# Row-tiled transposes of k and r, late logits with the gate weights stationary, and re-searched due dates in a one-core kernel

## The chip, the core and the metric

The kernel runs on one core of a Trainium2 chip. The core has five engines that work side by side, each through its own list of instructions in order: TensorE (PE in the profile; its weight loads are PEld), VectorE (DVE), ScalarE (ACT), GpSimd (POOL) and SyncE (SP, which issues transfers). PE writes its results to eight PSUM banks, and DVE and ACT copy them from there. The metric is the device time of one execution in microseconds (us); lower is better.

## The reference

Three parts follow one another: a linear attention with decay, a dense feed-forward layer with softplus, and a mixture of eight experts in which every expert takes exactly 384 tokens.

```python
batch, n_heads, seq, head_dim = (4, 8, 768, 48)
for t in range(S):
    cur = np.einsum('bhd,bhe->bhde', u[None] * kt, vt)
    y[:, :, t] = np.einsum('bhd,bhde->bhe', rt, state + cur)
    state = w[None, :, :, None] * state + np.einsum('bhd,bhe->bhde', kt, vt)

h = x @ w_in                                             # 3072 x 384 by 384 x 2048
g = np.maximum(h, 0.0) + np.log1p(np.exp(-np.abs(h)))
x = g @ w_out

logits = x @ w_gate                                      # 3072 x 8
for idx in np.argsort(-logits.flatten()):                # best pair of token and expert first
    tok, e = (int(idx) // E, int(idx) % E)
    if assigned[tok] >= 0 or counts[e] >= cap: continue
    assigned[tok] = e
    counts[e] += 1
for e in range(E):
    out[assigned == e] = np.maximum(x[assigned == e] @ w1[e], 0.0) @ w2[e]
```

`w_in` and `w_out` come as float64 and are converted on the core.

## The kernel before

The 3072 tokens are cut into 24 steps of 128 (two batches of 64 positions each) and into 8 blocks of three steps (384 tokens).

**Attention, one step** (`attention(n)`). k and r, scaled by powers of the decay, lie in `ks` and `rs` with 128 tokens on the partitions; each head has 48 values in a slot of 64, so two heads make 128 columns. PE transposes them head pair by head pair: `tk` (L591) and `tq` (L595) are four transposes of 128x128 each, into one bank each. A transpose is a matmul in which the data are the stationary operand, loaded by a weight load, and the identity is streamed. Copies take the banks to SBUF: `kT` in one copy, and `ar` in two of 64 partitions (for the first three steps, called direct, `rT` in one). Then `prods` (L618) multiplies k by r inside the step in 64x64 tiles of the array, `masked` (L628, DVE) writes the masked products into the free half of `ar`, `fresh` (L649) makes the step's own state in 64x64 tiles, and `outs` (L710, 128x64 tiles) gives the output. f32 matmuls appear as two records each in the trace, transposes as one.

**Feed-forward.** `ffn1` (L862 for block 0 in f32; L869 in f16 with three products of high and low halves) and the softplus on ACT and DVE fill `G`, high half `gh` and low half `gl`. `ffn2` (L980 for block 0; L983 to L985 later) multiplies by `w_out`. Behind its 384 columns `w_out` carries eight columns of the product w_out times w_gate (made through L813, L825 and L830), so that logits come out with the layer's output. For the last twelve token tiles (`LATE`, blocks 4 to 7) the output is computed late, beside the selection of experts, and their logits are computed ahead of it by `late_logits`: per token tile 32 matmuls with 128x128 of G stationary and 16 (L910) or 8 (L911) gate columns streamed, and two small DVE instructions that add the parts into `LG`.

**Experts.** `select` finds the tokens of one expert after another (L1235, L1252 and many DVE instructions), `gather` fetches them, `experts` runs L1476 (up) and L1494 to L1496 (down), and the results are scattered to the output.

**What sets the order.** Every piece of work is an `op` with an engine (or a choice of engines), an expected duration, what it reads and writes, a due date and, on PE, the banks that it takes. `lay_out` plays these through in the planner's own time: of the items that could start within `SLACK` of the earliest it takes the one with the smallest due date plus `NUDGE`; an item marked `small` is kept with others of that mark, and entering them costs `SWITCH`. `BIAS` and `YIELD` weigh one engine against another where there is a choice. `keep_warm` puts filler matmuls (L187) where the planner's PE is idle. What results is a fixed list for each engine; on the chip the engines wait for one another by semaphores alone.

Of the kernel before, what the change touches and what calls it, by code (L numbers as in the profile page):

```python
# [21 lines left out]
def tile_kernel(ctx, tc, r, k, v, w, u, w_in, w_out, w_gate, w1, w2, out):  # L22
# [33 lines left out]
    SLACK = 65.403  # L56
    SAME = {"dve": 130.0, "act": 150.0}
    NBANK = 7
    BIAS = 1.611999999999999
    YIELD0 = 221.503  # L60
# [498 lines left out]
    def attention(n):  # L559
# [27 lines left out]
        b1, b2 = Bank("att"), Bank("att")  # L587

        def tk():
            for pr in range(HP):  # L590
                PE.transpose(b1.view(HP, 128)[:, pr, :], ks[:, 2 * pr:2 * pr + 2, :].rearrange("p a d -> p (a d)"), identf)  # L591

        def tq():
            for pr in range(HP):
                PE.transpose(b2.view(HP, 128)[:, pr, :], rs[:, 2 * pr:2 * pr + 2, :].rearrange("p a d -> p (a d)"), identf)  # L595

        def qcopy(eng, q):
            copied(eng, ar[q * 64:(q + 1) * 64, :, :, q, :], b2.view(HP, 2, 64)[q * 64:(q + 1) * 64])

        op("pe", 437.0, tk, r=[("ks", i), "ident"], w=[("kT", i)], due=due + 2, bank=b1)  # L600
        op(FROM_BANK, 0.0, lambda eng: copied(eng, kT, b1.view(HP, 128)), w=[("kT", i)], due=due + 2, bank=b1)
        op("pe", 437.0, tq, r=[("rs", i), "ident"], w=[("ar", i, 0), ("ar", i, 1)], due=due + 2, bank=b2)
        if direct:
            op(FROM_BANK, 0.0, lambda eng: copied(eng, rT, b2.view(HP, 128)), w=[("ar", i, 0), ("ar", i, 1)], due=due + 2, bank=b2)
        for q in range(0 if direct else 2):
            op(FROM_BANK, 0.0, lambda eng, q=q: qcopy(eng, q), w=[("ar", i, q)], due=due + 2, bank=b2)

        b3 = [Bank("att"), Bank("att")]

        def prods():
            for pr in range(HP):
                for b in range(2):
                    for q in range(2):
                        rows, cols = slice(q * 64, (q + 1) * 64), slice(b * 64, (b + 1) * 64)
                        PE.matmul(b3[q].view(HP, 64)[cols, pr], kT[rows, pr, cols], rT[rows, pr, cols] if direct else ar[rows, pr, b, q, :],  # L618
                                  start=True, stop=True)
# [983 lines left out]
```

## Time and profile before

| | us |
|---|---|
| median of 3 runs | 736.38 |
| lowest and highest of them | 735.86 and 738.37 |
| the profiled execution | 735.12 |
| its span, first to last instruction | 733.4 |
| PE busy | 720.7 |
| DVE busy | 602.8 |
| ACT busy | 401.9 |

The mean granted TensorE clock is 0.993 of full. Matmuls are pipelined, so their busy time counts overlaps: what one costs the engine's list is read as the distance from its start to the start of the next. A timeline row merges neighbouring instructions of one kind: xcount says how many, the first number when the first of them began.

### The profile page before, as it was taken

The page shows a single profiled execution, that of the slowest core. Times are in us where ns is not written, and L with a number is a line of the kernel's source. Part 1 is how long each engine was busy: PE and PEld are TensorE (multiplying, and loading weights), DVE is VectorE, ACT ScalarE, POOL GpSimd, SP SyncE. Part 2 cuts the span into 40 slices and gives each one's busy share as a digit, 9 for nine tenths or more (in the row PEclk, how much of TensorE's full clock was granted, in tenths as well). Part 3 has the DMA queues.
Part 4 walks back from the last instruction along what each step waited for, and adds up shares of the span by engine and source line. Part 5 has one row for each costly group of instructions (what it writes and reads, how often), then busy time and mean ns, then how long its engine had stood idle before and what let it go on. Part 6 is the DMA issues. An engine that isn't in the chain of part 4 may idle for free.

```text
span 733.4 us, 18232 instructions
## 1 busy us (share of the span) xinstructions
PE 720.7 (98%) x7175; PEld 472.5 (64%) x7175; DVE 602.8 (82%) x1634; ACT 401.9 (55%) x826; POOL 65.1 (9%) x107
## 2 busy tenths in 40 slices
PE   9999999999999999999999999999998999999996
PEld 8986666666666666766666666666664665666663
DVE  6999999997999878698789858887797799978630
ACT  3697597752885399566899702220344433534531
POOL 3000000000000000000010000001212322312211
PEclk9999999999999999999999999999999999999998
DMA  7997833356635510060410003343247467647900
GB/s 149 230 197 190 229 102 56 67 108 123 112 61 99 97 31 15 15 107 1 67 23 2 2 12 109 108 141 93 76 124 227 132 173 199 203 122 210 269 33 32
DMA packets 165013, 79.65 MB, mean 109 GB/s; under 512 B 132800, under 2 KB 158272, under 8 KB 164928
## 3 DMA queue, kind: packets, MB, share of 16 engines
q1 hardware_dynamic: 159216, 68.56, 40.5%
q0 software_dynamic: 3072, 9.44, 3.8%
q8 instruction: 56, 0.92, 0.5%
q10 hardware_dynamic: 2640, 0.49, 0.4%
q14 instruction: 29, 0.24, 0.1%
HBM read 60.37 MB, written 9.83 MB: 96 GB/s over the span
## 4 chain that ended last, share of the span: by engine, by line
PE 73%; DVE 11%; issue 7%; ACT 4%; DMA 2%; POOL 1%; SPq 1%; another core or an unknown queue 0%; POOLq 0%; DVEq 0%
PE bank L869 19%; PE bank L1476 8%; PE bank L983 7%; PE bank L984 7%; PE bank L985 7%; PE bank L980 4%; PE bank L1494 2%; PE bank L1496 2%; PE bank L1495 2%; PE bank L710 2%; DVE ar L628 2%; DMA vn<-v 1%; PE bank L862 1%; PE bank L1235 1%; PE bank L618 1%
## 5 line engine op out<-in xcount | busy, mean ns | idle before, releaser
L869 PEld LDWEIGHTS <-wi 128*128 128x128 f16 x1008 | 98.2, 98 | 65.3 <-issue 1.5
L869 PE MATMUL bank<-xt,wi 128*128 128x384 f16 x672 | 127.6, 326 | 0.0
L983 PE MATMUL bank<-wo,g 128*128 128x384 f16 (+1 forms) x240 | 79.3, 331 | 0.0
L984 PE MATMUL bank<-wo,g 128*128 128x384 f16 (+1 forms) x240 | 79.1, 330 | 0.0
L985 PE MATMUL bank<-wo,g 128*128 128x384 f16 (+1 forms) x240 | 79.1, 330 | 0.0
L886 DVE SCALAR_TENSOR_TENSOR gf<-bank,ta 128x384 f32<-128x384 f32 x112 | 61.6, 554 | 15.7 <-ACT ta L881 15.1
L1476 PE MATMUL bank<-g,w1h 128*128 128x384 f16 x384 | 74.0, 329 | 0.0
L869 PE MATMUL bank<-xs,wi 128*128 128x384 f16 x336 | 72.9, 326 | 0.0
L880 ACT ACTIVATE ta<-ta 128x384 f32<-128x384 f32 x128 | 66.2, 519 | 1.8
L879 ACT ACTIVATE ta<-bank 128x384 f32<-128x384 f32 x128 | 61.3, 479 | 10.6 <-PE bank L869 6.3
L881 ACT ACTIVATE ta<-ta 128x384 f32<-128x384 f32 x128 | 65.9, 519 | 2.0
L1494 PE MATMUL bank<-w2h,g 128*128 128x384 f16 x192 | 62.6, 326 | 0.0
L1496 PE MATMUL bank<-w2h,g 128*128 128x384 f16 x192 | 62.6, 326 | 0.0
L1495 PE MATMUL bank<-w2l,g 128*128 128x384 f16 x192 | 62.5, 326 | 0.0
L424 ACT ACTIVATE x2o<-bank 128x384 f16<-128x384 f32 x24 | 11.6, 489 | 88.7 <-PE bank L985 54.0
L1480 ACT ACTIVATE g<-bank 128x384 f16<-128x384 f32 x64 | 31.2, 489 | 46.9 <-PE bank L1476 27.8
L1476 PEld LDWEIGHTS <-w1h 128*128 128x128 f16 x384 | 35.7, 98 | 23.0 <-issue 1.3
L893 DVE SCALAR_TENSOR_TENSOR g<-gf,g 128x384 f16<-128x384 f32 x80 | 43.5, 553 | 3.0 <-ACT g L424 2.0
L1483 DVE SCALAR_TENSOR_TENSOR g<-bank,g 128x384 f16<-128x384 f32 x64 | 34.6, 549 | 11.0 <-ACT g L1480 10.9
L1476 PE MATMUL bank<-g,w1l 128*128 128x384 f16 x192 | 42.2, 329 | 0.0
L1399 POOL DMA_INDIRECT third<-x2d,idx x24 | 26.7, 1111 | 154.0 <-DVE si L1314 128.4
L1429 ACT ACTIVATE w2h<-mraw 128x768 f16<-128x768 f32 x32 | 26.9, 841 | 22.6 <-DMA mraw<-moe_w 18.8
(251 smaller groups left out, 1442.8 us busy)
## 6 DMA issues: line engine op xcount, KB each, us to landing
mraw<-moe_w SPq DMA_DIRECT2D x64, 384.0 KB
third<-moe_w_out SPq DMA_DIRECT2D x8, 768.0 KB
third<-moe_w_in SPq DMA_DIRECT2D x6, 768.0 KB
x2d<-x2o SPq DMA_DIRECT2D x48, 96.0 KB
vn<-v SPq DMA_DIRECT2D x47, 96.0 KB
rn<-r SPq DMA_DIRECT2D x46, 96.0 KB
kn<-k SPq DMA_DIRECT2D x46, 96.0 KB
X<-v SPq DMA_DIRECT2D x36, 96.0 KB
```

What stands on the lines that cost most here:

```text
L869: PE.matmul(ph, WF[:, f, a, kk, :], x[:, kk, :], start=(i == 0), stop=(i == 3 * KC - 1))
L879: op("act", 371.0, lambda: ACT.activation(ta, bank.view(BT), AF.Abs), w=[("ta", c)], due=due, bank=bank)
L880: op("act", 413.0, lambda: ACT.activation(ta, ta, AF.Exp, scale=-1.0), w=[("ta", c)], due=due)
L881: op("act", 413.0, lambda: ACT.activation(ta, ta, AF.Ln, bias=1.0), w=[("ta", c)], due=due)
L886: op("dve", 470.0, lambda: DVE.scalar_tensor_tensor(gf, bank.view(BT), 0.0, ta, op0=OP.max, op1=OP.add), r=[("ta", c)], w=[("gf", c)], due ...
L983: PE.matmul(p, gh[:, f, ts], WU[:, f, 0, :no], start=(f == 0), stop=False)
L984: PE.matmul(p, gh[:, f, ts], WU[:, f, 1, :no], start=False, stop=False)
L985: PE.matmul(p, gl[:, f, ts], WU[:, f, 0, :no], start=False, stop=(f == FC - 1))
L1476: PE.matmul(ph, a[:, kk, fs], XH[p][:, x0 + kk, :], start=(i == 0), stop=(i == 3 * KC - 1))
L1494: PE.matmul(po, h1h[:, f, js], w2h[:, fz, :], start=(f == 0), stop=False)
L1495: PE.matmul(po, h1h[:, f, js], w2l[:, fz, :], start=False, stop=False)
L1496: PE.matmul(po, h1l[:, f, js], w2h[:, fz, :], start=False, stop=(f == FB - 1))
```

## The change

**Transposes.** Instead of four transposes of k and four of r, each 128x128, there are sixteen (`turned`, L597): for k and r, each head pair and each half of the rows (64 tokens of one batch). The two halves lie in different row tiles of the array and write different banks, and each bank holds both k and r. The four or three copies after them change with it: `kT` in two copies of 128x4x64, `ar` in two copies of 128x4x128, in which each r column is written twice (for the direct steps `rT` in two of 128x4x64). All sixteen are one item, marked `small`, which waits for `ks` and `rs`; `prods` waits for all four copies.

**Late logits.** Per block (three token tiles at once) the gate columns are stationary: `gates` puts them into `WGC`, 32 columns for each of the 16 pieces of w_out (eight high, eight low, the rest zero). 32 matmuls (L927) stream 384 columns of `gh` or `gl` each, in four column tiles of 32; ACT or DVE copies the 128x384 result to `LT`, three transposes (L932) turn it, and one DVE sum over the eight parts writes `LG`. `more_room` waits for this group too.

**Due dates.** `SLACK`, `BIAS`, `YIELD0` and all of `NUDGE` have new values (the table is cut here).

```diff
-    SLACK = 65.403
+    SLACK = 116.403
-    BIAS = 1.611999999999999
-    YIELD0 = 221.503
+    BIAS = 1.4120000000000001
+    YIELD0 = 267.503
-        1: -143624, 2: 51762, 4: 34057, 14: -25973, 15: 68285, 16: 100082, 17: 135695, 18: -1000120765, 19: -234504, 20: -202425, 21:
+        1: -91444, 3: 999869890, 4: -146263, 6: 999897800, 17: 150794, 42: -181722, 53: -229368, 54: -84025, 55: -53118, 56: -96415, 57:
...
-        b1, b2 = Bank("att"), Bank("att")
-
-        def tk():
-            for pr in range(HP):
-                PE.transpose(b1.view(HP, 128)[:, pr, :], ks[:, 2 * pr:2 * pr + 2, :].rearrange("p a d -> p (a d)"), identf)
...
-        def qcopy(eng, q):
-            copied(eng, ar[q * 64:(q + 1) * 64, :, :, q, :], b2.view(HP, 2, 64)[q * 64:(q + 1) * 64])
-
-        op("pe", 437.0, tk, r=[("ks", i), "ident"], w=[("kT", i)], due=due + 2, bank=b1)
-        op(FROM_BANK, 0.0, lambda eng: copied(eng, kT, b1.view(HP, 128)), w=[("kT", i)], due=due + 2, bank=b1)
-        op("pe", 437.0, tq, r=[("rs", i), "ident"], w=[("ar", i, 0), ("ar", i, 1)], due=due + 2, bank=b2)
...
+        kr = [Bank("att"), Bank("att")]
+
+        def turned():
+            for a, src in enumerate((ks, rs)):
+                for pr in range(HP):
+                    for b in range(2):
+                        rows = slice(b * 64, (b + 1) * 64)
+                        PE.transpose(kr[b].view(2, HP, 64)[:, a, pr, :], src[rows, 2 * pr:2 * pr + 2, :].rearrange("p a d -> p (a d)"),
+                                     identf[rows, rows])
+
+        def rcopy(eng, b):
+            r = kr[b].view(2, HP, 64)[:, 1]
+            if direct:
+                copied(eng, rT[:, :, b * 64:(b + 1) * 64], r)
+            else:
+                copied(eng, ar[:, :, b], r[:, :, None, :].to_broadcast([128, HP, 2, 64]))
+
+        op("pe", 500.0, turned, r=[("ks", i), ("rs", i), "ident"], w=[("kT", i), ("ar", i, 0), ("ar", i, 1)], due=due + 2, bank=kr, small=True)
+        for b in range(2):
+            op({"act": 375.0, "dve": 340.0}, 0.0, lambda eng, b=b: copied(eng, kT[:, :, b * 64:(b + 1) * 64], kr[b].view(2, HP, 64)[:, 0]),
+               w=[("kT", i, b)], r=[("kT", i)], due=due + 2, bank=kr[b])
...
-                PE.matmul(p, gh[:, f, ts], WU[:, f, :, DM:], start=(f == 0), stop=False)
-                PE.matmul(p[:, :E], gl[:, f, ts], WU[:, f, 0, DM:], start=False, stop=(f == FC - 1))
+        def mm(qs):
+            for q in qs:
+                for a in range(2):
+                    for j in range(4):
+                        PE.matmul(b1.view(m * 128)[32 * j:32 * j + 32], WGC[:, 4 * q + j].rearrange("p a e -> p (a e)"), G[g][a][:, 4 * q + j, ts],
+                                  start=(q == 0 and a == 0), stop=(q == FC // 4 - 1 and a == 1), tile_position=(0, 32 * j))
+
+        def tr():
+            for i in range(m):
+                PE.transpose(b2.view(m, 128)[:, i], LT[:, i * 128:(i + 1) * 128], identf)
...
+            op("pe", 330.0 * len(qs), lambda qs=qs: mm(qs), r=[(a, g, f) for a in ("gh", "gl") for y in qs for f in range(4 * y, 4 * y + 4)] + keys,
+               due=due_ffn1(blk, 4 * q + 4) + 500.0 if last else due, bank=b1, small=True)
+        op({"act": 413.0, "dve": 470.0}, 0.0, lambda eng: copied(eng, LT[:, :m * 128], b1.view(m * 128)), w=["lt", ("wi", FC)], due=due, bank=b1)
+        op("pe", 115.0 * m, tr, r=["lt", "ident"], due=due, bank=b2)
```

Three places in the lists. First PE, where a step's transposes stand behind the late part of `ffn2` (names: `third` and `g` are G, `identf` the identity, the number behind a bank's name its place). Before:

```order
L984 MATMUL bank_85<-wo,third 128x392
L985 LDWEIGHTS third
L985 MATMUL bank_85<-wo,third 128x392
L591 MATMUL bank_82<-identf,ks_102 128x128 x4
L595 MATMUL bank_86<-identf,rs_100 128x128 x4
L649 MATMUL bank_81<-vn_96,ks_103 64x48
```

After, behind another step's `outs`; of the sixteen the first two of k and the last two of r are shown:

```order
L716 MATMUL bank_85<-X_97,ar_112 64x48 x16
L597 MATMUL bank_82<-identf,ks_103 128x64
L597 MATMUL bank_83<-identf,ks_103 128x64
...
L597 MATMUL bank_82<-identf,rs_101 128x64
L597 MATMUL bank_83<-identf,rs_101 128x64
L1005 LDWEIGHTS g_128
L1005 MATMUL bank_80<-wo,g_128 128x392
```

Eight full transposes became eight pairs that alternate between two banks, and a third tile shape (64x128) stands between the shapes around it.

Then PE at the end of the last block's late logits, ahead of the late `ffn2`. Before:

```order
L910 LDWEIGHTS g_4951
L910 MATMUL bank_85<-wo,g_4951 128x16
L911 LDWEIGHTS g_4952
L911 MATMUL bank_85<-wo,g_4952 128x8
L983 LDWEIGHTS g_128
L983 MATMUL bank_84<-wo,g_128 128x384
```

After:

```order
L927 LDWEIGHTS wo
L927 MATMUL bank_85<-g_5019,wo 32x384
L932 MATMUL bank_81<-identf,wi 128x128 x3
L1005 LDWEIGHTS g_128
L1005 MATMUL bank_86<-wo,g_128 128x384
```

G was loaded and the gate columns streamed; now the gate columns are loaded and G is streamed, and the transposes of the result stand between the first matmuls of the late `ffn2`, six of them ahead of each of the last two blocks' three.

Last ACT, which makes most copies of the steps. Before (one step's three copies, other work between them):

```order
L430 COPY ar_111<-bank_81 64x8x64
L430 COPY kT_110<-bank_82 128x512
L430 COPY ar_111<-bank_81 64x8x64
L424 ACTIVATE x2o_132<-bank_85 128x384
L430 COPY ar_112<-bank_86 64x8x64
```

After:

```order
L433 COPY kT_110<-bank_83 128x4x64
L433 COPY ar_112<-bank_83 128x4x128
L433 COPY ar_112<-bank_82 128x4x128
L433 COPY kT_110<-bank_82 128x4x64
L427 ACTIVATE xhl<-xf_115 128x384
```

Three copies a step became four; the elements per partition are 1536 in both.

Counted over the whole lists: PE changes between tile shapes 102 times before and 136 times after; behind the first matmul of `ffn2` of block 0 (L980 before, L1002 after) 63 and 88 times. Of the 24 steps' transposes, 132 of 192 stand behind that matmul before, and 17 of 24 steps' after. Fillers: 154 before, 143 of them ahead of that matmul; 213 after, 203 ahead of it.

## Rows read from the trace of the kernel before

**Rows 1.** the page: busy time of each engine, its share and its instructions
```profile
PE 720.7 (98%) x7175; PEld 472.5 (64%) x7175; DVE 602.8 (82%) x1634; ACT 401.9 (55%) x826; POOL 65.1 (9%) x107
```

**Rows 2.** busy time in stretches (from:to, length, engines, clock, DMA share, GB/s)
```profile
60.00:80.00 20.00, 19.61 (x265) 13.81 (x265) 19.19 (x38) 15.25 (x33) 0.00 (x0) 1.00 0.79 205
80.00:100.00 20.00, 20.00 (x146) 12.69 (x145) 19.89 (x39) 13.94 (x34) 0.00 (x0) 1.00 0.79 181
...
120.00:140.00 20.00, 20.00 (x171) 12.17 (x168) 19.48 (x45) 14.82 (x34) 0.00 (x0) 1.00 0.31 58
...
420.00:440.00 20.00, 20.00 (x158) 12.23 (x157) 12.33 (x51) 0.49 (x1) 0.00 (x0) 0.95 0.04 11
...
540.00:560.00 20.00, 17.19 (x135) 10.37 (x134) 16.14 (x50) 7.04 (x11) 7.09 (x9) 0.96 0.56 179
560.00:580.00 20.00, 20.00 (x143) 11.81 (x141) 15.18 (x55) 8.27 (x13) 2.20 (x4) 0.95 0.49 129
...
700.00:720.00 20.00, 20.00 (x125) 12.04 (x124) 6.38 (x10) 6.59 (x12) 2.36 (x5) 1.00 0.06 20
```

**Rows 3.** waits of PE: line <- releaser: total us, times, longest
```profile
PE bank L1252 <- DVE fl L1247: 3.0, 2, 2.8
```

**Rows 4.** the chain that ended last, 33 to 95 us: start, us, what
```profile
69.01 0.96 DVE wo L778
```

**Rows 5.** timeline of PE, 180 to 184.5 us: start, us, line, xcount
```profile
180.49 0.60 PE L591 MATMUL bank<-identf,ks 128*128 128x128 f32 x4
180.93 0.33 PE L983 MATMUL bank<-wo,g 128*128 128x392 f16 x1
...
181.59 0.33 PE L984 MATMUL bank<-wo,g 128*128 128x392 f16 x1
181.75 0.33 PE L985 MATMUL bank<-wo,g 128*128 128x392 f16 x1
182.01 0.68 PE L649 MATMUL bank<-vn,ks 64*64 64x48 f32 x32
182.52 0.73 PE L618 MATMUL bank<-ar,kT 64*64 64x64 f32 x32
183.18 1.14 PE L710 MATMUL bank<-X,ar 128*64 128x48 f32 x32
```

**Rows 6.** the chain again, its longest pieces: the column sums L682
```profile
12.96 0.98 PE bank L682 x8
```

**Rows 7.** weight loads by form: busy us, mean ns, then idle time before
```profile
L618 PEld LDWEIGHTS bank<-ar,kT 64*64 64x64 f32 x768 | 13.7, 134 | 3.8 <-ACT ta L880 1.1 <-DVE gf L886 0.9 <-issue 0.8
...
L591 PEld LDWEIGHTS bank<-identf,ks 128*128 128x128 f32 x96 | 11.2, 141 | 2.2 <-DVE ar L628 0.6 <-issue 0.4
...
L682 PEld LDWEIGHTS bank<-uw,xhl 128*128 128x128 f32 x24 | 2.9, 191 | 0.1
```

**Rows 8.** timeline of PE, 76 to 79.3 us
```profile
76.50 0.86 PE L825 MATMUL bank<-third,gate 128*32 128x128 f32 x24
77.30 1.14 PE L710 MATMUL bank<-X,ar 128*64 128x48 f32 x32
...
78.97 0.60 PE L980 MATMUL bank<-wo,g 128*128 128x392 f32 x1
```

**Rows 9.** timeline of PE at the end of the late logits
```profile
418.48 0.17 PE L911 MATMUL bank<-wo,g 128*128 128x8 f16 x1
418.50 0.17 PE L910 MATMUL bank<-wo,g 128*128 128x16 f16 x1
...
419.63 0.53 PE L983 MATMUL bank<-wo,g 128*128 128x384 f16 x1
419.95 0.53 PE L984 MATMUL bank<-wo,g 128*128 128x384 f16 x1
```

**Rows 10.** copies of ACT out of a bank, by form
```profile
L430 ACT COPY kT<-bank 128x512 f32<-128x512 f32 x22 | 12.8, 583 | 10.5 <-PE bank L591 10.4
...
L430 ACT COPY third<-bank 128x128 f32<-128x128 f32 x4 | 1.1, 263 | 2.0 <-ACT third L430 1.0 <-PE bank L825 0.9
```

More of the change, by code (lines that the diff above doesn't have):

```diff
@@ L584, in attention @@
         am = flat_ar[:, HP * 128:].rearrange("p (q a t) -> p q a t", q=2, a=HP)
-        b1, b2 = Bank("att"), Bank("att")
-        def tk():
-            for pr in range(HP):
-                PE.transpose(b1.view(HP, 128)[:, pr, :], ks[:, 2 * pr:2 * pr + 2, :].rearrange("p a d -> p (a d)"), identf)
-        def tq():
-            for pr in range(HP):
-                PE.transpose(b2.view(HP, 128)[:, pr, :], rs[:, 2 * pr:2 * pr + 2, :].rearrange("p a d -> p (a d)"), identf)
-        def qcopy(eng, q):
-            copied(eng, ar[q * 64:(q + 1) * 64, :, :, q, :], b2.view(HP, 2, 64)[q * 64:(q + 1) * 64])
@@ L600, in attention @@
-        op("pe", 437.0, tk, r=[("ks", i), "ident"], w=[("kT", i)], due=due + 2, bank=b1)
-        op(FROM_BANK, 0.0, lambda eng: copied(eng, kT, b1.view(HP, 128)), w=[("kT", i)], due=due + 2, bank=b1)
-        op("pe", 437.0, tq, r=[("rs", i), "ident"], w=[("ar", i, 0), ("ar", i, 1)], due=due + 2, bank=b2)
[L603 to L606, printed above, removed]
+        kr = [Bank("att"), Bank("att")]
@@ new lines, in attention @@
+        op("pe", 500.0, turned, r=[("ks", i), ("rs", i), "ident"], w=[("kT", i), ("ar", i, 0), ("ar", i, 1)], due=due + 2, bank=kr, small=True)
+        for b in range(2):
+            op({"act": 375.0, "dve": 340.0}, 0.0, lambda eng, b=b: copied(eng, kT[:, :, b * 64:(b + 1) * 64], kr[b].view(2, HP, 64)[:, 0]),
+               w=[("kT", i, b)], r=[("kT", i)], due=due + 2, bank=kr[b])
+        for b in range(2):
+            op({"act": 375.0, "dve": 340.0} if direct else FROM_BANK, 0.0, lambda eng, b=b: rcopy(eng, b),
+               w=[("ar", i, 0, b)], r=[("ar", i, 0), ("ar", i, 1)], due=due + 2, bank=kr[b])
@@ L611, in attention @@
+        kTs, ars = [("kT", i)] + [("kT", i, b) for b in range(2)], [("ar", i, q) for q in range(2)] + [("ar", i, 0, b) for b in range(2)]
         b3 = [Bank("att"), Bank("att")]
@@ L629, in masked @@
                                mask[rows, None, :].to_broadcast([64, HP, 64]))
-        op("pe", 625.0, prods, r=[("kT", i), ("ar", i, 0), ("ar", i, 1)], w=[("am", i, 0), ("am", i, 1)], due=due + 3, bank=b3, small=True)
+        op("pe", 625.0, prods, r=kTs + ars, w=[("am", i, 0), ("am", i, 1)], due=due + 3, bank=b3, small=True)
         for q in range(2):
@@ L676, in attention @@
         if n < TURNED:
-            op("dve", 602.0, lambda: DVE.tensor_tensor(rkT, rT if direct else b2.view(HP, 128), kT, op=OP.mult),
-               r=[("kT", i)] + ([("ar", i, 0)] if direct else []), w=["rkT"], due=due + 3, bank=None if direct else b2)
+            op("dve", 602.0, lambda: DVE.tensor_tensor(rkT, rT, kT, op=OP.mult),
+               r=kTs + ars, w=["rkT"], due=due + 3)
             def sums():
@@ L713, in attention @@
         if direct:
[L714 removed]
+            op("pe", 2000.0 if n % PC else 650.0, outs, r=[("am", i, 0), ("am", i, 1)] + ars + vnk
                + ([("st", x, 0), ("st", x, 1), ("xv", x, 0), ("xv", x, 1)] if n % PC else []), w=[("xf", i)], due=due + 4 + OUTL, bank=b55, small=True)
         else:
[L717 removed]
+            op("pe", 1069.0, outs, r=[("am", i, 0), ("am", i, 1)] + ars + [("st", x, 0), ("st", x, 1)]
                + [("xv", x, q) for q in range(2)], w=[("xf", i)], due=due + 4 + OUTL, bank=b5, small=True)
@@ L898, in tile_kernel, with gates @@
     lgs = []
+    WGC = WU[:, FC].rearrange("p a m -> p (a m)")[:, :FC * 32].rearrange("p (f a e) -> p f a e", f=FC, a=2)
+    LT = WF[:, FC].rearrange("p a k f -> p (a k f)").bitcast(FT)
+    def gates():
+        due = due_ffn2(1, 0, FC - 1)
+        keys = ["wgc", ("wo", FC), ("wg", FC)]
+        op("dve", 200.0, lambda: DVE.memset(WGC, 0.0), r=[("wol", FC - 1)], w=keys, due=due)
+        for a in range(2):
+            op("dve", 200.0, lambda a=a: DVE.tensor_copy(WGC[:, :, a, :E], WU[:, :FC, a, DM:]),
+               r=["wgc"] + [(k, f) for k in ("wo", "wg", "wol") for f in range(FC)], w=[("wgc", a)], due=due)
@@ L900, in late_logits @@
     def late_logits(blk, t):
-        g = SLOT[blk]
-        ts = slice(t * 128, (t + 1) * 128)
-        bank = Bank("sel")
+        g, m = SLOT[blk], SPB - t
+        ts = slice(t * 128, BT)
+        b1, b2 = Bank("sel"), Bank("sel")
         GROUP[0] = "late"
-        def mm(q):
-            p = bank.view(2 * E)
-            gh, gl = G[g]
-            for f in range(4 * q, 4 * q + 4):
-                PE.matmul(p, gh[:, f, ts], WU[:, f, :, DM:], start=(f == 0), stop=False)
-                PE.matmul(p[:, :E], gl[:, f, ts], WU[:, f, 0, DM:], start=False, stop=(f == FC - 1))
+        def mm(qs):
+            for q in qs:
+                for a in range(2):
+                    for j in range(4):
+                        PE.matmul(b1.view(m * 128)[32 * j:32 * j + 32], WGC[:, 4 * q + j].rearrange("p a e -> p (a e)"), G[g][a][:, 4 * q + j, ts],
+                                  start=(q == 0 and a == 0), stop=(q == FC // 4 - 1 and a == 1), tile_position=(0, 32 * j))
@@ L913, in put @@
+        def tr():
+            for i in range(m):
+                PE.transpose(b2.view(m, 128)[:, i], LT[:, i * 128:(i + 1) * 128], identf)
         def put():
-            g = LG[:, blk * SPB + t, :]
-            DVE.tensor_copy(g, bank.view(2 * E)[:, :E])
-            DVE.tensor_tensor(g, bank.view(2 * E)[:, E:], g, op=OP.add)
+            DVE.tensor_reduce(LG[:, blk * SPB + t:(blk + 1) * SPB, :],
+                              b2.view(m, 8, 16).rearrange("p m x e -> p m e x")[:, :, :E], axis=AX.X, op=OP.add)
@@ L918, in late_logits @@
         last = blk == NB - 1
-        for q in range(FC // 4):
-            due = due_ffn1(blk, 4 * q + 4 if last else FC) + 500.0
-            it = op("pe", 200.0, lambda q=q: mm(q), r=[(a, g, f) for a in ("gh", "gl") for f in range(4 * q, 4 * q + 4)],
-                    due=due, bank=bank)
-            if not last:
-                it.deps += [writer[a, g, FC - 1] for a in ("gh", "gl")]
-        lgs.append(op("dve", 270.0, put, due=due, bank=bank))
+        due = due_ffn1(blk, FC) + 500.0
+        keys = [("wgc", a) for a in range(2)]
@@ new lines, in late_logits @@
+        for q in range(FC // 4 if last else 1):
+            qs = [q] if last else range(FC // 4)
+            op("pe", 330.0 * len(qs), lambda qs=qs: mm(qs), r=[(a, g, f) for a in ("gh", "gl") for y in qs for f in range(4 * y, 4 * y + 4)] + keys,
+               due=due_ffn1(blk, 4 * q + 4) + 500.0 if last else due, bank=b1, small=True)
+        op({"act": 413.0, "dve": 470.0}, 0.0, lambda eng: copied(eng, LT[:, :m * 128], b1.view(m * 128)), w=["lt", ("wi", FC)], due=due, bank=b1)
+        op("pe", 115.0 * m, tr, r=["lt", "ident"], due=due, bank=b2)
@@ L928, in tile_kernel @@
+        lgs.append(op("dve", 300.0, put, due=due, bank=b2))
     BIG = 1.0e38
@@ L1043, in tile_kernel @@
                 halve_wout(f)
+            gates()
             users = [it for a, k in (("raw", 4), ("wtmp", 3), ("wgt", 4)) for i in range(k)
@@ L1051, in tile_kernel @@
             ffn1(blk, f)
-        for t in range(SPB):
-            if (blk, t) in LATE:
-                late_logits(blk, t)
+        first = min([t for b, t in LATE if b == blk], default=None)
+        if first is not None:
+            late_logits(blk, first)
     GROUP[0] = "sel"
@@ L1117, in tile_kernel @@
     spacer = None
-    more_room = Item("none", 0.0, make_more_room, [room] + [it for it in items if it.group == "ffn"], begins(NB))
+    more_room = Item("none", 0.0, make_more_room, [room] + [it for it in items if it.group in ("ffn", "late")], begins(NB))
     chain = []
```

2 lines of the change are left out of this document (removed), and 57 rows, old and new, of the table NUDGE.

## The prediction

> **What bounds the kernel now.** I read the page's busy table and its strips first, then the busy time in stretches of 20 us, then TensorE's waits, then the chain. PE is busy for 720.7 of 733.4 us [rows 1] and 20.00 of 20 us in 25 of the 32 stretches between 80 and 720, 17.19 in the worst [rows 2]. The waits say the same: the longest thing PE waited for, by name, is 3.0 us [rows 3]. So from about 79 us, where the first L980 matmul of block 0 starts [rows 8], to the last matmul the kernel is a queue of PE work without holes, and a microsecond taken out of that queue is a microsecond of the end. Ahead of 79 us it is otherwise: DVE is busy for 19.19 of 20 us [rows 2] and the chain runs through DVE's conversions of the float64 weights [rows 4], while PE burns time in filler matmuls (L187). What PE saves there shows as more filler, not as time.
>
> "Busy" is the wrong measure for a sum: matmuls overlap, so one of 0.33 us costs 0.16 us of the queue [rows 5]. All terms below are distances from start to start.
>
> **Transposes (gain).** Before, four f32 transposes of 128x128 take 0.44 us (180.49 to 180.93), 0.11 each [rows 5]. Of 192, 132 stand behind the first L980: 132 x 0.11 = 14.5 us. The change issues 16 per step, as eight pairs; the two of a pair sit in different row tiles. Each streams 64 columns of the identity instead of 128, and loads 64 rows by 128 columns. No row shows this form. Nearest are L649 and L618, four tiles of 64x64 at a time: 32 records in 0.51 us (182.01 to 182.52), 0.064 per four [rows 5]. Tiles thus load and stream side by side there, over rows and over columns.
>
> What that row leaves open is the load, which has 64 columns there and 128 here. Two rows bound it. An f32 load of 128 columns alone sets the pace in L682, whose matmuls stream two columns each: 8 records in 0.98 us, 0.12 each [rows 6]. And the load records: 191 ns for L682, 134 for L618, but 141 for the transposes L591, with the same 128x128 shape as L682 [rows 7]. A transpose's load is recorded almost as short as one of 64 columns, so I take the pace of the 64x64 tiles: 8 x 0.064 = 0.51 us per step, 17 steps behind the first L980: 8.7 us. **Minus 5.8 us.** Ends: 0.44 per step (half of 8 x 0.11) gives minus 7.0; 0.12 per pair gives 0.98 per step, 16.6 us, plus 2.1.
>
> The Trainium skill (TensorE: Matmul & The Clock Gate, section "LDWEIGHTS (loading the stationary operand)") says that a load's time goes by its columns and not by its rows, P / 1.2 in ns; an estimate from it is 107 ns for 128 columns, however few rows. By that a pair would take 107 ns, a step 0.86, and the term would be about zero; the 112 to 122 ns of L682 agree with it, the short record of L591 speaks against it for transposes. This is the first rival.
>
> **Changes of tile shape (loss).** The 16 are a shape of their own (64x128) between 128x128, 64x64 and 128x64 work. Going from full to 64x64 costs 0.26 instead of 0.16 (181.75 to 182.01), 0.10 more; L618 to L710 costs 0.66 instead of 0.51, 0.15 more [rows 5]. I take 0.12. The list of PE has 63 such changes behind the first L980 before, 88 after: 25 x 0.12 = **plus 3.0 us** (2.5 to 3.7).
>
> **Late logits (gain).** Before, 12 token tiles x 32 matmuls, one each 0.025 us (418.48 to 418.50) [rows 9]: 384 x 0.025 = 9.6 us. After, four blocks x 32 matmuls of 384 columns in four column tiles, so eight rounds per block if four go together, plus three transposes. L825 shows four column tiles of 32: 24 records in 0.80 us (76.50 to 77.30), six rounds, with the change of shape at its end [rows 8]; (0.80 - 0.12) / 6 = 0.113 per round, the price of one transpose of 128 columns. So four cost what one costs. A round here streams 384 f16 columns, 0.16 us for one [rows 5], say 0.17; 4 x (8 x 0.17 + 3 x 0.11) = 6.8 us. **Minus 2.8 us** (shape changes are counted above). If the four took turns: 128 x 0.16 + 1.3 = 21.8, plus 12.2.
>
> **The clock behind them.** After the last 192 narrow matmuls TensorE runs at 1.2 GHz: ten L983 to L985 stand 0.32 apart instead of 0.16 [rows 9], and 420 to 440 us has a clock of 0.95 [rows 2]. That is 1.6 us. In the change streams of 384 columns stand there. I cannot tell whether the fall goes away; half: **minus 0.8 us** (0 to minus 1.6). The other such stretch, 560 to 580 [rows 2], lies among the experts, which are not touched; it stays in the sum.
>
> **Off PE.** A step had three ACT copies of 512 elements, 583 ns each for the one of kT; it has two of 512 and two of 256 now. 256 lies between 263 ns (128) and 583 (512) [rows 10], about 0.37: 2 x 0.37 + 2 x 0.58 = 1.9 instead of 1.74 us. ACT is busy 55% of the span [rows 1], so the 0.17 hides, unless prods, which stands behind four copies instead of three, comes up on PE too soon (second rival). In the changed list 2 to 7 us of PE work stand between the transposes of a step and its prods, at the paces above (22 in one step). In DVE's list the first w_out conversion is row 132 before and after, so I leave the 79 us where they are, give or take 1.5. The 59 more fillers say that PE idles more there, as it must with less to do; they fill time that DVE sets, and cost nothing. The late chain (copy, transposes, one sum) is about 1 us longer before selection can start, but PE goes on into 12 tiles of L983 to L985, over 90 us, and its wait there is nil; hidden. The re-searched due dates move much and remove nothing by themselves: PE has no holes to close.
>
> **Sum** against the profiled run (735.12, of which 733.4 are the span): -5.8 + 3.0 - 2.8 - 0.8 = -6.4, so 728.7. The runs' median stands 1.26 above that profiled run; I add half: **729.3 us**.
>
> **Rivals.**
> 1. The transposes' loads set the pace: a pair takes 0.11 to 0.12 us. For it: L682's pace. Against: L591's load record. Term plus 0.5 to 2.1 in place of minus 5.8: 735.0 to 736.6 on the profiled run, about 736 to 737: no change. Chance 0.13.
> 2. New holes: prods or masked products wait on the four copies, or DVE, at 19.5 of 20 us between 120 and 140 [rows 2], cannot keep up with a shorter PE queue. 0.2 to 0.3 us in each of 17 steps, 3.4 to 5: about 733 to 734. Against it: the distances above, and DVE's spare time behind 140 us. Chance 0.07.
> 3. Slower: the two row tiles take turns, since each fills all 128 columns, which no row of before shows side by side. 16 x 0.11 = 1.76 us per step, 30 us, plus 15.4: 735.12 + 15.4 + 3.0 - 2.8 - 0.8 = 749.9, 750.5 as a median. It decides from about 1.0 us per step. Against it: L618, where two of the four tiles share their columns and still go together [rows 5]. Chance 0.05.
> 4. The late logits' four tiles take turns: 15 us more than my term, about 744. L825 speaks against it. Chance 0.03.
>
> **How the numbers follow.** My forecast has 0.72, the rivals 0.13, 0.07, 0.05 and 0.03. A measurement here tells about 0.3% (2.2 us) from no change, so faster means below 734.2. Faster: 0.72 + 0.06 of rival 2 = 0.78. Same: rival 1 and the rest of 2, 0.14. Slower: rivals 3 and 4, 0.08. Low end: all terms at their good ends (-7.0, +2.5, -1.6, 1.5 off the start) make 724.7; 724.5. The high end takes in rival 2 and most of rival 1: 736.5. My forecast's own range is 724.5 to 733.
>
> **What would show it.** In the profile after: pairs of the transposes' records a few ns apart, 0.06 from pair to pair (rival 1: 0.11; rival 3: singles); late rounds 0.17 apart; no clock of 0.95 around the end of the late logits; the first L1002 matmul (L980 before) at 77.5 to 80.5 us; PE without named waits above 3 us. Wrong would be: a first L1002 well behind 80 us, PE waiting on ACT copies in the steps, or new stretches at 1.2 GHz, where short tiles follow one another.

## The result, and the profile after

The changed kernel took 723.83 us (723.49 to 725.28), the kernel before 736.19 us (735.47 to 738.37) beside it: ratio 0.983, 95% interval 0.981 to 0.985. That is 12.4 us, where I had forecast 6.9, and 0.7 us below the low end of my range. On three other chips the kernel before took 731.6 to 733.0 us (medians and single executions), and on two of them the changed kernel 723.0 (one execution) and 724.1, the latter at a ratio of 0.989 (0.987 to 0.991): 8.9 us. Both numbers need an explanation, and so does the difference between them.

The page of the changed kernel, beside [rows 1]:

```profile
PE 712.3 (99%) x7182; PEld 461.2 (64%) x7182; DVE 598.6 (83%) x1615; ACT 398.9 (55%) x859; POOL 67.4 (9%) x107
```

Its busy time in stretches, in the columns of [rows 2] (the clock stands behind the POOL column):

```profile
420.00:440.00 20.00, 20.00 (x171) 12.51 (x170) 12.40 (x51) 0.98 (x2) 0.00 (x0) 1.00 0.09 20
540.00:560.00 20.00, 20.00 (x169) 12.46 (x167) 19.17 (x55) 10.99 (x18) 6.60 (x7) 1.00 0.71 168
560.00:580.00 20.00, 20.00 (x137) 11.95 (x136) 16.72 (x59) 10.24 (x17) 6.32 (x9) 1.00 0.76 204
```

In all three the clock is 1.00 where [rows 2] had 0.95, 0.96 and 0.95, and the stretch from 540 has 20.00 us of PE in place of 17.19. The longest waits of PE, against the 2.8 us of [rows 3]:

```profile
PE bank L190 <- DVE ar L513: 1.0, 1, 1.0
PE bank L551 <- POOL X L583: 0.5, 1, 0.5
PE bank L597 <- DVE gf L892: 0.4, 1, 0.4
```

Cut at four places of PE's queue, and measured there from start to start, the spans stand like this (the first pair of traces is that of the result; the second was taken later on another chip, both kernels one behind the other):

| us, from the trace | before | after | before, 3rd trace | after, 3rd trace |
|---|---|---|---|---|
| first matmul of block 0's second product (L980, L1002) starts at | 78.97 | 79.67 | 78.78 | 80.17 |
| from there to the end of the late-logits matmuls (L911, L927) | 339.74 | 334.35 | 340.22 | 332.89 |
| from there to the first expert matmul (L1476, L1499) | 106.93 | 105.13 | 107.99 | 105.12 |
| from there to the last matmul | 200.75 | 195.95 | 195.85 | 196.08 |

The second and third lines are the change, and the first line takes 0.7 and 1.4 us of it back. The last line, the experts, gains 4.8 us in the first pair and nothing in the second. My forecast had taken the 200.75 as given.

### The profile page after: what moved, and what is told of

Read it like the earlier page. It is cut to its first block, busy times and chain, and to the rows that moved or that the text cites. A ratio compares the mean times of both kernels' runs of the same rounds, so it can differ in the third digit from the quotient of the medians.

```text
span 722.1 us, 18256 instructions
## 1 busy us (share of the span) xinstructions
PE 712.3 (99%) x7182; PEld 461.2 (64%) x7182; DVE 598.6 (83%) x1615; ACT 398.9 (55%) x859; POOL 67.4 (9%) x107
## 4 chain that ended last, share of the span: by engine, by line
PE 76%; DVE 10%; issue 8%; ACT 2%; POOL 2%; DMA 1%; POOLq 0%; SPq 0%; DVEq 0%; ACTq 0%
PE bank L875 15%; PE bank L1499 9%; PE bank L1005 7%; PE bank L1007 7%; PE bank L1006 7%; PE bank L868 5%; PE bank L1002 3%; PE bank L1517 3%; PE bank L1519 3%; PE bank L1518 3%; PE bank L716 2%; PE bank L597 2%; PE bank L624 2%; PE bank L655 1%; DVE ar L634 1%
## 5 line engine op out<-in xcount | busy, mean ns | idle before, releaser
L1499 PE MATMUL bank<-g,w1h 128*128 128x384 f16 x384 | 72.8, 326 | 0.0
L1499 PEld LDWEIGHTS <-w1h 128*128 128x128 f16 x384 | 35.4, 97 | 22.1
L1499 PE MATMUL bank<-g,w1l 128*128 128x384 f16 x192 | 41.7, 326 | 0.0
L1452 ACT ACTIVATE w1h<-mraw 128x768 f16<-128x768 f32 x32 | 26.7, 838 | 22.3 <-DMA mraw<-moe_w 18.5
```

What stands on the lines that cost most here:

```text
L1499: PE.matmul(ph, a[:, kk, fs], XH[p][:, x0 + kk, :], start=(i == 0), stop=(i == 3 * KC - 1))
```

## The new forms run as forecast

PE's timeline at one step of the changed kernel, the transposes of k and of r (start, us, line):

```profile
68.95 0.46 PE L597 MATMUL bank<-identf,ks 64*128 64x64 f32 x8
69.25 0.41 PE L597 MATMUL bank<-identf,rs 64*128 64x64 f32 x8
69.59 0.59 PE L868 MATMUL bank<-xt,wi 128*128 128x384 f32 x1
```

Sixteen transposes take 0.64 us with the changes of shape at both ends. The records of a pair lie 3 to 4 ns apart, and one pair follows the other after 61 to 64 ns, the second pair of a step after 111: but for that one, the pace that I took from L618 and L649 (0.064). Their loads, by form:

```profile
L597 PEld LDWEIGHTS bank<-identf,ks 64*128 64x128 f32 x192 | 8.3, 138 | 3.8 <-DVE rs L422 0.6 <-ACT X L433 0.6 <-DVE g L889 0.5
```

A load of 64 rows by 128 columns has a record of 138 ns, the transposes' load of before one of 141 [rows 7]. The Trainium skill (TensorE: Matmul & The Clock Gate, section "LDWEIGHTS (loading the stationary operand)") has a load's time go by its columns; an estimate from its figure is 107 ns for 128. The records here are longer than that, and yet a pair with 128 columns per load follows the one before after 62 ns. So the time of a load doesn't set the pace of these transposes, and my first rival is out.

The end of the late logits in the changed kernel; L932 turns the sums back:

```profile
412.29 1.80 PE L927 MATMUL bank<-g,wo 128*32 128x384 f16 x40
414.02 0.55 PE L932 MATMUL bank<-identf,wi 128*128 128x128 f32 x3
414.40 0.33 PE L1005 MATMUL bank<-wo,g 128*128 128x384 f16 x1
414.56 0.33 PE L1006 MATMUL bank<-wo,g 128*128 128x384 f16 x1
```

Forty matmuls in ten rounds of four take 1.73 us to the next line, 0.17 a round, as forecast. And the two matmuls behind them are 0.16 apart, where [rows 9] had 0.32.

## Experiments: each form undone

**Whole transposes in the new order.** A bank takes two pairs of heads instead of one half of the tokens; the order on every engine is that of the changed kernel.

```diff
-                    for b in range(2):
-                        rows = slice(b * 64, (b + 1) * 64)
-                        PE.transpose(kr[b].view(2, HP, 64)[:, a, pr, :], src[rows, 2 * pr:2 * pr + 2, :]..., identf[rows, rows])
+                    PE.transpose(kr[pr // 2].view(2, 2, 128)[:, a, pr % 2, :], src[:, 2 * pr:2 * pr + 2, :]..., identf)
```

> The changed kernel with one part undone: k and r are again transposed as eight whole 128x128 matmuls per step in place of sixteen in two row tiles; each bank takes two pairs of heads where it took one half of the tokens, the four copies keep their size, and the order on every engine is the same. Theory (the row tiles run beside each other and are paid back in part by tile-shape changes): the 24 steps' transposes go from 11.7 to about 15.1 us in the sum over PE's starts, and the tile-shape changes around them give about 0.6 back: +2.8 us (2.2 to 3.4) on the changed kernel's 723.8, so about 726.6, 0.987 of before. Rival (the pair costs what one whole transpose costs, and the gain came with the new order): within 0.5 us of 723.8, 0.983.

Measured: 728.63 us, 0.995 of before (0.994 to 0.997), against 0.989 for the changed kernel: 4.7 us by the ratios, 3.9 by the spans (726.3; the changed kernel's second trace has 722.4). The transposes, in sums by form:

```profile
L595 PE MATMUL bank<-identf,ks 128*128 128x128 f32 x96 | 15.3, 282 | 0.0
```

From start to start they take 15.9 us between the first matmul of block 0's second product and the late logits (17 steps), 11.9 in the changed kernel's second trace; 1.1 of these 4.1 us come back in the matmuls around them, as the tile shape changes less often. Minus 3.0 there, where my sum had -5.8 + 3.0 = -2.8. Another 0.9 us is lost ahead of that matmul, which starts at 81.16 us here and at 80.29 there. In all this is more than the 2.2 to 3.4 us that I had expected of this run. The rival is refuted. The run takes back only 14 of the 25 added changes of shape (counted in the traces), so it doesn't price all 25.

**Narrow late logits in the new order.** G is loaded and the gate columns streamed, in the new items' places; the result is copied and added, with no turn.

```diff
-                        PE.matmul(b1.view(m * 128)[32 * j:32 * j + 32], WGC[...], G[g][a][:, 4 * q + j, ts], ..., tile_position=(0, 32 * j))
+                    PE.matmul(p, gh[:, f, ti], WU[:, f, :, DM:], start=(f == 0 and i == 0), stop=False)
+                    PE.matmul(p[:, :E], gl[:, f, ti], WU[:, f, 0, DM:], start=False, ...)
```

> The changed kernel with the other part undone: the late logits again as narrow matmuls (G loaded, 16 and 8 gate columns streamed), in the places where the new ones stood; the turn of the result by transposes falls away, the copy is smaller, one addition takes the place of the reduction. The order on every engine is else the same. By form alone: the late logits go from 5.4 + 1.4 (their transposes) to about 9.7 us, +2.9, so about 726.7, 0.987 of before. Theory: the narrow matmuls also bring back the fall of the granted clock to 1.2 GHz behind the last block's late logits (near 415 us here), for about 3 us, which costs another 1.5: about 728.2, 0.989, with a slice under 1.0 there. Rival: the fall at 420 in the kernel before had to do with its order, not with the narrow matmuls: no slice under 1.0, 726.7.

In this first build the columns in which a block's sums wait are used again before they have been added, so two blocks take the next block's logits and their tokens go to other experts; the work is the same in kind and amount. Measured: 728.68 us, 0.9955 (0.994 to 0.997). The second build gives each block its own columns:

> The changed kernel with the late logits as narrow matmuls again, each block's result in columns of its own; else as the run before of this kind. By form the late logits cost 2.9 us more, and behind the last block's the granted clock falls to 1.2 GHz for some 3 us (1.5 us): theory +4.4 on the changed kernel, 728.2 (727.5 to 729). Rival: the clock doesn't follow the narrow matmuls, +2.9.

Measured: 729.39 us, 0.9957 (0.994 to 0.997), a little above the expected 727.5 to 729, with the changed kernel beside it at 0.9888: 5.1 us. The matmuls take 9.94 us from start to start, against 5.43 and 1.42 for the turns: 3.1 by form. The rest is mostly the clock; the stretches of this kernel:

```profile
400.00:420.00 20.00, 20.00 (x365) 14.96 (x364) 13.61 (x30) 14.88 (x36) 0.00 (x0) 0.91 0.01 2
420.00:440.00 20.00, 20.00 (x157) 12.10 (x154) 11.13 (x45) 0.69 (x2) 0.00 (x0) 0.92 0.05 11
440.00:460.00 20.00, 20.00 (x158) 12.13 (x157) 15.96 (x67) 4.35 (x6) 0.00 (x0) 1.00 0.29 91
```

From 420.35 to 422.91 us eight matmuls of 384 columns stand 0.32 apart instead of 0.16: 1.3 us. All ten traces in which the last narrow matmuls stand 192 or 288 in a row (4.8 to 7.4 us), in the old order and in the new, have such a stretch right behind them, 7 to 16 matmuls long, 1.1 to 2.5 us; the six traces with streamed G have none, nor has the one kernel whose narrow matmuls stand at most 96 in a row (the old items under the new table, below). So in the traces the fall of the clock to 1.2 GHz comes with the long row of narrow matmuls and goes with it, and the theory holds.

Two things on record limit it. In the first build the clock also fell behind a row of 96 (340.84 to 343.25 us), the only one of 18 such rows in these traces:

```profile
340.00:360.00 20.00, 20.00 (x248) 14.10 (x246) 13.85 (x31) 17.12 (x42) 0.00 (x0) 0.91 0.06 12
```

And not every execution of the kernel before seems to have the fall. Of its 61 timed executions on the three other chips, eight (729.0 to 730.5 us) had a mean granted clock of 0.998, as the changed kernel's have (0.997 to 0.999), and the other 53 had 0.991 to 0.996. None of the eight was traced.

**Both undone in the new order.**

> The changed kernel with both forms undone, whole transposes and narrow late logits, in the new order: what the new search is worth by itself. Theory (the two forms are the whole gain, and add up): 724.0 + 4 to 4.7 (whole transposes) + 4.4 to 5.3 (narrow late logits) = 732.4 to 734, 1.000 +- 0.002 of before. Rival (the new order gains by itself): 729 to 730, 0.995, or the two share part of their gain.

Measured: 732.65 us, 1.002 of before (1.000 to 1.003). By the ratios both together are worth 9.4 us (1.002 against 0.989), the parts 4.7 + 5.1 = 9.8: they add up, and the new order by itself gains nothing.

## Experiments: the new due dates

The old table put onto the new items, and the new table onto the old items, each number to the counterpart of its item:

```diff
-    SLACK = 116.403
+    SLACK = 65.403
...
     NUDGE = {
-        1: -91444, 3: 999869890, ...
+        1: -143624, 2: 51762, ...
```

> The changed kernel with the old search: every due date that the old table shifts is shifted by the same amount here (each item of the old kernel has its counterpart in the new one; the second transpose item of a step and the third addition of the late logits have none), and the old slack, bias and yield. So the two new forms alone, in an order that was not searched for them. Theory (the forms carry the gain, the search only keeps the other engines out of PE's way): PE's own work is the same, so what it loses against the changed kernel is waits alone: 0 to 5 us, 724 to 729, 0.990 to 0.995. Rival (the new search is what gained): at or above the kernel before, 732 or more.

> The kernel before with the new table of due dates, slack, bias and yield, each item shifted as its counterpart in the changed kernel: the search alone, without the two new forms. Theory (the forms carry the gain): no faster than before, 0 to 5 us slower, 732 to 737, 1.000 to 1.007. Rival (the new due dates gain by themselves): 3 us or more below before, under 729, 0.996 or less.

Measured: 737.50 us, 1.008 (1.006 to 1.011), and 799.89 us, 1.094. My theory misses both. The new forms in an order that was not searched for them are slower than before, as the rival had it (732 or more), by 13.5 us against the changed kernel. In the span they lose early (block 0's second product starts at 84.85 us), in the middle (339.1 us, for 334.1) and in the experts (198.1 us). 8.3 us of it stand in the filler matmuls, which are laid where the planner itself expects PE to idle: 24.6 us of them against 16.3, from start to start. The 5.0 us of the middle are not fillers; what they are stays open.

```profile
L160 PE MATMUL bank<-still 128*128 128x128 bf16 x348 | 26.4, 234 | 1.0 <-DVE ar L483 1.0
```

In the other kernel the late products are drawn forward, out of the time in which selection runs, and the fillers there and among the experts grow by 58 us. So a table of this kind goes with the items it was searched for. The new forms need the new one, and with the old forms in its order it gains nothing over the old one; my "re-searched due dates move much and remove nothing by themselves" holds.

## Experiments: the hole among the experts

The first trace of before has PE standing 2.8 us at L1252, for DVE's flag. DVE came late to L1341 there, and ACT to L1480, though PE's products for them had ended at 553.95 and 555.43 us. DVE, ACT and POOL in the first trace of before (start, us, line, idle time before it):

```profile
557.08 0.17 DVE L1341 COPY tok<-bank 64x12 f32<-64x12 f32 x1 [2.87 <-remote]
...
557.23 0.49 ACT L1480 ACTIVATE g<-bank 128x384 f16<-128x384 f32 x1 [1.20 <-remote]
...
552.53 1.08 POOL L1399 DMA_INDIRECT third<-x2d,idx  x1 [0.31 <-issue]
553.92 1.12 POOL L1399 DMA_INDIRECT third<-x2d,idx  x1 [0.30 <-issue]
555.34 0.95 POOL L1399 DMA_INDIRECT third<-x2d,idx  x1 [0.30 <-issue]
```

The semaphore events of the trace put PE's two signals at 557.05 and 557.15 us, 3.1 and 1.7 us behind the products. Eleven signals of PE are 0.4 us or more late in that trace, some 16 in the first trace of the changed kernel, all among the experts and while GpSimd issues an indirect transfer or within 0.4 us of its end. (Three of the eleven and most of the 16 have no event of their own in the trace; they are taken to have come with the next one.) Is this the kernel's or the execution's?

> The kernel before, unchanged, profiled a second time, to see whether what the first profile showed between 540 and 580 us belongs to this kernel or to that one execution. Theory: the hole belongs to the order of this kernel. PE's digit product L1252 waits 2 to 3 us again near 555 us for DVE's flag, DVE's copy L1341 stands just before it although its product L1336 has ended, and the granted clock falls to 1.2 GHz twice, for some 3 us near 420 (behind the late logits) and near 560 (behind the hole); span 733 +- 1. Rival: the hole was a chance of one execution. Then L1252 waits under 1 us there, only the stretch at 420 is left, and the span is 4.4 us shorter, about 729.

> The kernel before, unchanged, profiled a third time, on whatever chip comes. Theory (the late signals of PE belong to some chips or executions): with late signals (0.4 to 3.1 us between the end of a PE product and its semaphore) the span is 733 or more and a wait of PE over 1 us stands in the expert stage; without any, the expert stage takes 195.9 us as in the second trace. Rival (the hole at 555 us is part of this kernel): the wait of 2.8 us at L1252 shows without a late signal.

> The changed kernel, unchanged, beside the kernel before on the chip on which the kernel before has just taken 732.0 us, and where its second trace shows no wait of 2.8 us at L1252 and no late signal of PE: its expert stage takes 195.9 us there, as the changed kernel's did in its first trace (195.95). Theory: the 4.8 us that the expert stage seemed to gain were the hole of the one trace of before, and belong to the executions of that chip, not to the change; what the change gives is the middle stage (5.4 to 6.8) and the clock behind the late logits (1.8): 723.5 to 724.8, ratio 0.988 to 0.990. Rival: the new order is worth the 4.8 us anywhere: ratio 0.983 again, 719.6.

> The changed kernel, unchanged, profiled a third time on the same chip. Without late signals: expert stage 195.9 us, span 722 +- 1. With late signals, theory: they fall where PE has other work queued, as in the first trace (16 of them, and 195.95 us), or open a wait of 1 to 3 us, since nothing in this order keeps room for them; the span is 722 to 727.

Measured: the kernel before 732.26 and 731.57 us, the changed kernel 724.05 (five rounds, 0.989, 0.987 to 0.991) and 723.02. No signal of PE is late in these four traces; the expert stage takes 195.86, 195.85, 195.87 and 196.08 us. The second trace of before, its stretches and its longest waits of PE:

```profile
420.00:440.00 20.00, 20.00 (x181) 12.30 (x178) 12.61 (x54) 0.49 (x1) 0.00 (x0) 0.91 0.03 6
540.00:560.00 20.00, 20.00 (x161) 12.23 (x161) 18.94 (x55) 9.23 (x15) 7.08 (x9) 1.00 0.63 187
560.00:580.00 20.00, 20.00 (x143) 11.92 (x141) 16.24 (x63) 8.65 (x14) 2.96 (x5) 1.00 0.66 169
```
```profile
PE bank L649 <- DMA vn<-v: 1.7, 1, 1.7
PE bank L187 <- DVE ar L510: 1.0, 1, 1.0
```

The hole and the clock's dent at 560 are gone, the dent behind the late logits is there. My theory, that the hole belongs to the order, fell here, and with it the rival of the result, that the new order is worth 4.8 us anywhere.

**The lateness made by hand.** Three idle comparisons on DVE ahead of L1341 (L1364 after), on chips without late signals:

```diff
         def invert_d():
+            if p == 3:
+                for _ in range(3):
+                    against(z["cmi"], TB["slot"], 64, z["sd"][:, 1])
```

> The kernel before with three idle comparisons (0.96 us each) ahead of DVE's copy L1341 of expert 3: they write a tile that has just been used up, so nothing else changes, and DVE comes about 2.87 us late to that copy, as it did in the first trace of before, where PE's signal was late. Theory (the hole of that trace and its fall of the clock come from this one lateness): PE waits 2.8 us at the digit product behind it, the granted clock falls to 1.2 GHz for about 3.4 us (1.6 us): +4.4 on before, 1.006. Rival (DVE has room there, or the clock fell for another reason): +2.8 without the clock, or 0 to 1.

Measured: 735.82 us, 1.006 (1.004 to 1.008), +4.1. The first trace is there again, with 200.24 us in the expert stage; timeline of PE:

```profile
554.93 0.65 PE L1479 MATMUL bank<-g,w1l 128*128 128x384 f16 x3
558.39 0.18 PE L1252 MATMUL bank<-fl,onu 128*128 128x8 bf16 x1 [2.81 <-DVE fl L1247]
558.43 1.44 PE L1479 MATMUL bank<-g,w1h 128*128 128x384 f16 x6
559.66 1.17 PE L1479 MATMUL bank<-g,w1l 128*128 128x384 f16 x3
```

and in stretches:

```profile
540.00:560.00 20.00, 17.19 (x137) 10.32 (x136) 18.93 (x53) 7.14 (x12) 7.68 (x9) 0.98 0.57 179
560.00:580.00 20.00, 20.00 (x140) 11.88 (x139) 15.18 (x55) 8.18 (x13) 2.20 (x4) 0.94 0.50 129
```

**The same, with PE kept busy**, by 40 zero matmuls ahead of that digit product:

> As the run before, and PE multiplies a zero tile 40 times (128 columns, 0.056 us each, 2.2 us) ahead of that digit product, in the time in which it would stand. Theory (the clock falls because PE stood): the clock stays at 2.4 GHz, only the wait is left: +2.8 on before, 1.004, and 1.6 less than the run before. Rival (the fall has another cause): as the run before, +4.4.

Measured: 733.75 us, 1.003 (1.001 to 1.005), 2.1 us less than the run before. The expert stage takes 198.66 us, 2.8 more than without the lateness, and its clock stays whole, with 0.6 us of the wait left:

```profile
PE bank L1255 <- DVE fl L1247: 0.6, 1, 0.6
```
```profile
560.00:580.00 20.00, 19.43 (x144) 11.68 (x145) 16.55 (x59) 7.67 (x13) 2.20 (x4) 1.00 0.53 151
```

So the clock fell because PE stood, and the fall costs 1.6 us on top of the wait's 2.8.

**The same lateness in the changed kernel.**

> The changed kernel with the same three comparisons ahead of the same copy (L1364 here) of expert 3. Its digit product follows 0.5 us behind DVE's flag in the trace of its second run (flag at 545.3 to 545.5, product at 546.04 us). Theory (the new order has no more room there; it was spared by chance of where PE's signals came late): PE waits 2.3 to 2.4 us, the clock falls: +3.5 to 4.0 on the changed kernel's 724, 0.994 of before. Rival (the new order covers such lateness, which would make the 4.8 us of the expert stage a gain of the change): 0 to +1, 0.989 to 0.990.

Measured: 726.92 us, 0.993 (0.990 to 0.995), against 0.989: +2.8 by the ratios, and 199.85 us in the expert stage, +4.0.

```profile
PE bank L1275 <- DVE fl L1270: 2.1, 1, 2.1
```
```profile
540.00:560.00 20.00, 17.86 (x142) 10.59 (x140) 18.38 (x47) 9.38 (x15) 7.97 (x7) 0.91 0.51 158
```

The 4.0 hold 2.1 us of wait and, in this trace, a fall of the clock. The other five executions had a mean granted clock of 0.997 to 0.999, as without the lateness (0.995 in the traced one), so there the wait seems to have come without the fall; that fits the 2.8. The new order has little more room there than the old one. In its first trace the late signals fell where PE had other work queued: luck, not a gain of the change.

**The gathers held back.** One copy of an index makes the three gathers of expert 2 wait:

```diff
         def one(j):
+            if p == 2 and j == 0:
+                POOL.tensor_copy(spacer, IDX[3][0:1, 0:1])
```

> The kernel before with one small instruction more: GpSimd copies one number of the index tile of expert 3 ahead of its three gathers for expert 2, so that these gathers start after the index tile has been written, some 3 us later than before (they stood at 552.5 to 556.3 us; their rows are wanted at 561.6 at the earliest). All else keeps its order. Theory: PE's signals of 553.95 and 555.43 reached DVE and ACT 3.1 and 1.6 us late because the gathers were being issued; with the gathers gone from there the signals come at once, PE's wait of 2.8 us at L1252 goes, the clock does not fall behind it (1.6 us): -4.4 us, about 731.8, 0.994 of before; the late signals move with the gathers to a place where PE has work queued. Rival: the late signals have another cause, and the hole stays: 736.2, 1.000. Between: the late signals follow the gathers and open a smaller hole behind it (-1 to -3).

> The kernel before with the three gathers for expert 2 held back until the index tile of expert 3 is written, once more, on the same chip. Where late signals of PE show in the two runs beside it, theory (they come while GpSimd issues indirect transfers): none between 552 and 557 us, and the wait at L1252 is gone; rival: the wait stays. Where none show, the run tells nothing new: expert stage 195.9 us, as before.

Measured: 732.09 us, 0.999 (0.998 to 1.001), and 735.65 in a single run. Neither trace has a late signal, nor have the traces of the unchanged kernel on those chips, so these runs say nothing on the question; the expert stage is 195.86 us in both. Holding the gathers back costs nothing, and that is all. What the single run has more than the third trace of before lies ahead of the gathers: its late logits end 4.5 us later, behind two more falls of the clock (0.91 in the first 20 us, and 0.91 from 180 to 200 us, behind a wait of 1.2 us).

## Why the prediction was right in sign and short in size

- **PE as a queue without holes:** right, with one exception that I had on the table. [rows 2] showed 17.19 of 20 us, and [rows 3] the 2.8 us. I wrote that the stretch "lies among the experts, which are not touched; it stays in the sum". This is the step that failed: 4.8 us that belonged to one execution (2.8 of wait, 1.6 of clock, the rest small) went into the base as if the kernel owned them. On the other three chips that stage took 195.9 us in both kernels, and 2.8 us of lateness made by hand brought the 200.2 back. In the first comparison the changed kernel had late signals too, but lost nothing by them, so the hole counted as a gain. The five times of before there, 735.5 to 738.4 us, stand some 4 us above the medians on the three other chips; that all had such a hole fits, but only one execution there, of 735.1 us, was traced.
- **Transposes and tile shapes:** -5.8 + 3.0 forecast behind the first L1002, -3.0 measured there. The pairs' pace was right. That the two terms come out together is in part luck: the transposes by themselves gained less than I had (4.1 of 5.8), since the slower start and the shape changes of a step show within their own sum (0.70 us a step, where I had 0.51), and outside it 1.1 us showed, for 14 of the 25 changes, where I had 3.0 for all.
- **Late logits:** -2.8 forecast, -3.1 by form.
- **Clock behind them:** half of 1.6 forecast; in the traces it goes away whole, 1.1 to 2.5 us. What varies is the kernel before, in which some executions seem to have no fall.
- **Early part:** the first L1002 at 79.67, 80.29 and 80.17 us, inside my 77.5 to 80.5, but 0.7 to 1.4 us later than before, where I had zero. Ahead of it the transposes take 2.5 us less and the fillers 3.0 us more, or somewhat over. I wrote that fillers cost nothing there, as DVE sets the time; PE waits for nothing longer than 1.0 us in these traces, so that isn't shown.
- **Copies and prods (second rival):** no wait of PE on a copy over 0.4 us; hidden.
- **Median over the profiled run:** the half that I added (0.6) pointed the wrong way.

Against a trace of before without the hole (its run 731.6 to 732.3 us) my -6.4 gives 725.2 to 725.9; 723.0 to 724.1 was measured. What is left is the clock's other half and more, less what the early part lost, and scatter of about a microsecond between executions of before, some of it a wait for v's load (1.7 us at L649 in the second trace).

What stays open is why PE's signals came late. They coincide with GpSimd's indirect transfers, but the same transfers in the same places, on three other chips, held up none.

## What to carry to other kernels

A wait in a trace that no work explains (an engine idle, though its input's producer had ended) may belong to that execution: take a second trace of the kernel before, and price a change on the base without it. A hole on PE costs its length and can cost the slow clock behind it: the wait of 2.8 us was worth 4.4. Put matmuls of a few columns into column tiles and stream the long side: here the form gained 3.1 us, and the clock behind it stayed up in all six traces.

## What the runs showed of the hardware

- PE's granted clock fell to 1.2 GHz behind 2.8 us in which PE stood, in one traced execution behind 2.1 us, and behind one of four waits of 1.2 to 1.7 us at L649. It stayed at 2.4 GHz where zero matmuls filled the wait of 2.8 us.
- It also fell in the course of, or right behind, 4.8 to 7.4 us of narrow matmuls (16 and 8 columns, 0.025 us apart) that followed one another without a gap, in all ten traces that have them, and behind one of 18 rows of 96 (2.4 us). The matmuls of 384 columns behind the long rows then stood 0.32 us apart instead of 0.16, for 2.2 to 5.1 us.
- f32 transposes of 64 rows in two row tiles went in pairs, 62 ns from pair to pair, although each load has 128 columns and a record of 138 ns.
- Semaphore signals of PE reached DVE and ACT up to 3.1 us behind the product's end on one chip, in the traces of both kernels; on three others, in 15 traces, none came late among the experts.
